# One token block of the forward gated layer moved from the first stage to the second

## The chip, the cores and the metric

The kernel runs on one core of a Trainium2 chip. A core has a matrix engine (TensorE, PE in the profile), a vector engine (VectorE, DVE), a scalar engine (ScalarE, ACT), GpSimd (POOL) and SyncE (SP), each with its own in-order queue of instructions, and 16 DMA engines. PEld is TensorE's weight load, which overlaps its matmuls. The metric is the device time of one execution in microseconds (us), taken as the median of several runs.

## The reference

The kernel computes a forward pass and all its gradients in one launch. S = 2048 tokens, D = 512 channels, F = 1376 hidden columns, bfloat16.

```python
x = A_q;  xn = layernorm(x)
# A: shift convolution, then a long causal convolution over the tokens
k_shift = sum over t < 4 of k[s - t] * shift_k[:, t]
kv = k_shift * v
y  = fft_conv(kv, ssm_k) + kv * ssm_D
s  = xn * y
# B: gated layer
g = xn @ w_gate;  u = xn @ w_up
h = sigmoid(g) * u
z = h @ w_down
out = x + s * silu(z)
# returned: out, and the gradients of A_q, A_k, A_v, shift_k, ssm_k, ssm_D,
#           w_gate, w_up, w_down for a given grad_out
```

## The kernel before

The 2048 tokens are 16 blocks of 128, numbered 0 to 15: token p*16 + j is partition p of block j. The long convolution works on four groups (cg) of 128 channels, each over all tokens, as dense Fourier matrices.

**Stage A** runs four streams side by side: `strG`, the forward part of the gated layer for the token blocks in the list `FA` (L34); and for each channel group `strK` (transform of the filter), `strV` (shift convolution and transform of kv) and `strX` (product and inverse transform, which gives y). `run_streams` (L519, called at L996) merges them into one program order by progress: `strG` is to run from 5% to 70% of the stage, with a total of `len(FA) * 11776` columns.

A forward block, `f_gen(i)` (L719), is 88 matmuls of 128x128 by 128 columns in three parts, each part followed by a sigmoid on ScalarE and a multiply on VectorE out of PSUM. On the way it loads, normalizes and transposes later blocks: `f_x` (three places ahead), `f_ln` (two), `f_xnT` (one, four transposes). Its results h and sigma are 352 KB each.

**Stage B** (`stepB`, L1133) takes the token blocks 0 to 15 in order. For each it does the down projection and the gates (`z_gen`, L1054), the gradient of the hidden layer (`d_gen`, L1085) and of x (`x_gen`, L1110); and, where block i + 3 was not in `FA`, that block's `f_gen` as well. Of the blocks done in stage A the last three (`LAG`, L30) stay in SBUF; the others, `NSP` of them, are written to DRAM at the end of `f_gen` and read back by `f_ld` (L752) in stage B. All of h and the two hidden gradients are also transposed by DMA and stored for the weight gradients.

**Stage C** runs the backward convolution (`frontC`, `backC`) beside the weight gradients (`dW`, L1189), which are 35 accumulations over the 16 token blocks that depend on nothing in stage C and also run alone at the end.

The order on the engines isn't the program order: `Rec.order` (L352) collects all operations with their dependencies, and places them one by one in the queue of their engine by estimated durations and by their number in the program; operations with two forms, the copies out of PSUM (`evac`, L241) and the normalization, go to ScalarE or VectorE as it finds them free. So an edit of the program order makes a new order of everything behind it. Because all operations are emitted by one line, every row of the profile names L515.

The lines that the change touches, and what depends on them:

```python
FA = [14, 13, 12, 11, 9, 7, 5, 4, 0, 1, 2]             # L34
NSP = len(FA) - LAG                                     # L35
SEQ = FA + [i for i in range(NJ) if i not in FA]        # L36: order of all forward blocks
POS = {i: n for n, i in enumerate(SEQ)}                 # L37
...
if n < NSP:                                             # L747, end of f_gen
    nc.gpsimd.dma_start(hF_d[n]..., hT)
    nc.gpsimd.dma_start(sF_d[n]..., sigT)
...
f = f_gen(i + LAG) if i + LAG < NJ and i + LAG not in FA else iter(())   # L1136, stepB
...
if i + LAG in FA[:NSP]:                                 # L1151
    f_ld(i + LAG)
```

Of the kernel before, what the change touches and what calls it, by code (L numbers as in the profile page):

```python
# [30 lines left out]
LATE = 0.25  # L31
SURE = 0.6
AHEAD = 500
FA = [14, 13, 12, 11, 9, 7, 5, 4, 0, 1, 2]  # L34
NSP = len(FA) - LAG  # L35
SEQ = FA + [i for i in range(NJ) if i not in FA]  # L36
POS = {i: n for n, i in enumerate(SEQ)}  # L37
# [481 lines left out]
def run_streams(streams, until=None):  # L519

    live = [list(st) + [0.0] * (5 - len(st)) for st in streams]
    while live:
        if until is not None and until():
            break
        for st in sorted(live, key=lambda s: s[2] + (s[3] - s[2]) * s[4] / s[1]):
            try:
                c = next(st[0])
            except StopIteration:
                live.remove(st)
                break  # L530
            if c:
                st[4] += c
                break
        else:
            raise RuntimeError("all streams blocked")
    return live
# [75 lines left out]
def kernel_impl(ctx, tc, A_q, A_k, A_v, A_shift_k, A_ssm_k, A_ssm_D, B_x, B_w_gate, B_w_up, B_w_down,  # L612
# [106 lines left out]
    def f_gen(i):  # L719
        n = POS[i]  # L720
        if n == 0:
            f_xnT(i)
            yield 512
        xnT = T[i]["xnT"]
        if n + 3 < NJ:
            f_x(SEQ[n + 3])
        sigT, hT = sig_r.next(), h_r.next()
        T[i]["sig"], T[i]["h"] = sigT, hT
        for pi, (f0, nb) in enumerate(FBS):
            if PS["wide"]:  # L730
                ps = ps_mm([2, 4, 128], name="psGU")
                pg, pu = ps[:, 0], ps[:, 1]
            else:
                pg, pu = ps_mm([4, 128], name="psG")[:], ps_mm([4, 128], name="psU")[:]
            for pt_, w in ((pg, wg), (pu, wu)):
                for b in range(nb):
                    for db in range(4):
                        nc.tensor.matmul(pt_[:, b, :], w[:, db, (f0 + b) * 128:(f0 + b + 1) * 128], xnT[:, db, :],
                                         start=(db == 0), stop=(db == 3))
            nc.scalar.activation(sigT[:, f0:f0 + nb, :], pg[:, 0:nb, :], ACT.Sigmoid)  # L740
            nc.vector.tensor_tensor(hT[:, f0:f0 + nb, :], pu[:, 0:nb, :], sigT[:, f0:f0 + nb, :], ALU.mult)
            if pi == 0 and n + 2 < NJ:
                f_ln(SEQ[n + 2])
            if pi == 1 and n + 1 < NJ:
                f_xnT(SEQ[n + 1])
            yield nb * 1024 + (512 if pi == 1 else 0)
        if n < NSP:  # L747
            nc.gpsimd.dma_start(hF_d[n].rearrange("p (a t) -> p a t", t=128), hT)
            nc.gpsimd.dma_start(sF_d[n].rearrange("p (a t) -> p a t", t=128), sigT)
        token_major(hT, hS_d[i])  # L750

    def f_ld(i):  # L752
        n = POS[i]
        sigT, hT = sig_r.next(), h_r.next()
        T[i]["sig"], T[i]["h"] = sigT, hT
        nc.gpsimd.dma_start(hT, hF_d[n].rearrange("p (a t) -> p a t", t=128))
        nc.gpsimd.dma_start(sigT, sF_d[n].rearrange("p (a t) -> p a t", t=128))
# [66 lines left out]
    def strG():  # L824
        for n, i in enumerate(FA):
            if n > 0:
                run_pend(2)
            yield from f_gen(i)
# [81 lines left out]
    def strK():  # L910
        for cg in range(NG):
            KT = stA.pop(("KT", cg))
            nc.vector.tensor_tensor(KT[:, 0:1], KT[:, 0:1], Dcol_b[:, cg:cg + 1], ALU.add)
            KC = KC_r.next()
            for jh in range(2):
                pt = ps_tr([8, 128], name="ps_kt")
                for jj in range(8):
                    nc.tensor.transpose(pt[:, jj, :], KT[:, 8 * jh + jj:S:16], ident)
                nc.evac(KC[:, 8 * jh:8 * jh + 8, :], pt[:], 1024)
                yield 1024  # L920
            if cg + 1 < NG:
                ld_KT(cg + 1)
            Qg = QgK_r.next()
            yield from step1(lambda j: KC[:, j, :], Qg)
            while cg > 1 and ("s3K", cg - 2) not in flags:
                yield 0
            Qf = QfK_r.next()
            yield from flip(Qg, Qf)
            stA["QfK", cg] = Qf
            flags.add(("flK", cg))  # L930

    def strV():
        for cg in range(NG):
            kh, vg = stA["kh", cg // 2], stA["vg", cg // 2]
            lc = (cg % 2) * GW
            c0, c1 = cg * GW, (cg + 1) * GW
            acc = acc_r.next()
            for lag in (3, 2, 1, 0):
                src = kh[:, 3 - lag: 3 - lag + NJ, lc:lc + GW]
                skl = skb[:, lag:lag + 1, c0:c1].to_broadcast([P, NJ, GW])  # L940
                if lag == 3:
                    nc.vector.tensor_tensor(acc, src, skl, ALU.mult)
                else:
                    term = term_r.next()
                    nc.vector.tensor_tensor(term, src, skl, ALU.mult)
                    yield 1024
                    nc.vector.tensor_tensor(acc, acc, term, ALU.add)
                yield 1024
            nc.gpsimd.dma_start(ksh_d[cg], acc.rearrange("p j d -> p (j d)"))
            kvt = kvt_r.next()  # L950
            nc.vector.tensor_tensor(kvt, acc, vg[:, :, lc:lc + GW], ALU.mult)
            if cg == 1:
                ld_k(1)
                ld_v(1)
            yield 1024
            Qg = QgV_r.next()
            yield from step1(lambda j: kvt[:, j, :], Qg)
            while cg > 0 and ("s3V", cg - 1) not in flags:
                yield 0
            Qf = QfV_r.next()  # L960
            yield from flip(Qg, Qf)
            stA["QfV", cg] = Qf
            flags.add(("flV", cg))

    def strX():
        yield from gen_ci()
        for cg in range(NG):
            while ("flK", cg) not in flags:
                yield 0
            QfK = stA.pop(("QfK", cg))  # L970
            KFg = KFg_r.next()
            for qq in range(4):
                yield from step3(QfK, qq, X_RI, KFg[:, qq])
                nc.gpsimd.dma_start(KK_d[cg, qq, :, 0], KFg[:, qq])
            flags.add(("s3K", cg))
            while ("flV", cg) not in flags:
                yield 0
            QfV = stA.pop(("QfV", cg))
            Bg = Bg_r.next()
            ys = {}  # L980
            for qq in range(5):
                if qq < 4:
                    Xc, Xs, Y = Xc_r.next(), Xs_r.next(), Y_r.next()
                    yield from step3(QfV, qq, X_RI, Xc)
                    nc.gpsimd.dma_start(KK_d[cg, qq, :, 1], Xc)
                    nc.vector.tensor_tensor(Y, Xc, KFg[:, qq], ALU.mult)
                    yield from step3(QfV, qq, X_IR, Xs)
                    nc.vector.tensor_tensor(Xs, Xs, KFg[:, qq], ALU.mult)
                    ys[qq] = ((Y, R_A), (Xs, R_B))
                    if qq == 3:  # L990
                        flags.add(("s3V", cg))
                if qq > 0:
                    yield from inv3(ys.pop(qq - 1), qq - 1, Bg)
            yield from inv1(Bg, y2A[:, :, cg * GW:(cg + 1) * GW])

    run_streams([(gG, len(FA) * 11776, 0.05, 0.7), (strK(), 4 * 10240, 0.0, 0.7), (strV(), 4 * 16384, 0.0, 0.8),  # L996
                 (strX(), 4 * 24576 + 4096, 0.2, 1.0)])
# [27 lines left out]
    def b_ld(i):  # L1025
        T[i]["x"], T[i]["go"] = xq2_r.next(), go_r.next()
        nc.gpsimd.dma_start(T[i]["x"], qC[:, i, :])
        nc.gpsimd.dma_start(T[i]["go"], goC[:, i, :])
# [104 lines left out]
    def stepB():  # L1133
        yield from z_gen(0)
        for i in range(NJ):
            f = f_gen(i + LAG) if i + LAG < NJ and i + LAG not in FA else iter(())  # L1136
            d, x = d_gen(i), x_gen(i)
# [11 lines left out]
            if i + 2 < NJ:  # L1149
                b_ld(i + 2)  # L1150
            if i + LAG in FA[:NSP]:  # L1151
                f_ld(i + LAG)
# [299 lines left out]
```

## Time and profile before

| | us |
|---|---|
| median of 5 runs | 557.92 (557.53 to 563.25) |
| the profiled execution | 557.02 |
| its span, first to last instruction | 555.1 |
| stage A, to the first matmul of token 0's backward | 176.4 |
| TensorE busy in the span | 525.3 |
| VectorE busy | 442.9 |
| ScalarE busy | 354.7 |
| mean granted TensorE clock | 0.999 |

The span is what the profile covers; the profiled execution's own time is 1.9 us longer, and 0.9 us under the median. "Busy" of TensorE counts overlapping matmuls as one stretch, so 95% busy isn't 95% of its peak. Stretches of time are counted from the first instruction; each operation of the program can be found in the trace by its place in its engine's queue.

### The profile page before, as it was taken

The numbers are of one execution on the slowest core, as the hardware profiler recorded it, in microseconds if no ns is written. First come the engines' busy times: TensorE is split into PE (matmuls) and PEld (weight loads), VectorE is DVE, ScalarE is ACT, GpSimd is POOL, SyncE is SP. The second block draws the span as 40 slices with busy tenths as digits, with TensorE's granted clock in tenths as the row PEclk, the third lists the DMA queues.
The fourth block names the chain that finished last, engine by engine and source line by source line (L and its number), as shares of the span: only waits on it lengthen the run. The fifth ranks groups of instructions, "written<-read, shape, count | busy, mean of one in ns | idle before, by whom it ended". The sixth has DMA issues, their size and how long they took to land.

```text
span 555.1 us, 13618 instructions
## 1 busy us (share of the span) xinstructions
PE 525.3 (95%) x5548; PEld 377.0 (68%) x5613; DVE 442.9 (80%) x869; ACT 354.7 (64%) x463; POOL 143.9 (26%) x254
## 2 busy tenths in 40 slices
PE   3987999999989999999999999999999999999996
PEld 2986998898868666667755665656756746667444
DVE  9599999957877999989899899648669798898510
ACT  7979999978986434354433444368848759775211
POOL 3243425303222122222232110310241051421221
PEclk9999999999999999999999999999999999999999
DMA  8978988967352899979999999998596369687431
GB/s 288 247 213 241 329 217 280 202 194 236 113 181 73 181 242 203 234 163 256 210 264 264 257 228 259 320 293 220 192 295 214 136 201 322 201 258 250 150 113 37
DMA packets 125608, 121.81 MB, mean 219 GB/s; under 512 B 75027, under 2 KB 104553, under 8 KB 125546
## 3 DMA queue, kind: packets, MB, share of 16 engines
q1 hardware_dynamic: 109946, 71.22, 51.8%
q0 software_dynamic: 15072, 49.72, 28.0%
q8 instruction: 44, 0.72, 0.5%
q14 instruction: 18, 0.15, 0.1%
q10 hardware_dynamic: 528, 0.00, 0.0%
HBM read 54.95 MB, written 48.27 MB: 186 GB/s over the span
## 4 chain that ended last, share of the span: by engine, by line
PE 67%; DVE 14%; issue 9%; ACT 6%; POOL 2%; DMA 2%; POOLq 0%; ACTq 0%; DVEq 0%
PE psum L515 67%; DVE slab L515 14%; ACT slab L515 6%; DMA out_dram<-slab 2%; POOL out_dram L515 1%; POOL slab L515 0%; ACT L515 0%; POOLq L1447 0%; POOLq L515 0%; ACTq L515 0%; DVEq L515 0%; POOLq L1436 0%
## 5 line engine op out<-in xcount | busy, mean ns | idle before, releaser
L515 PE MATMUL psum<-slab 128*128 128x128 bf16 (+4 forms) x5548 | 525.3, 255 | 25.4 <-ACT slab L515 12.7
L515 PEld LDWEIGHTS <-slab 128*128 128x128 bf16 (+3 forms) x5613 | 377.0, 102 | 173.3 <-issue 20.3
L515 DVE TENSOR_TENSOR slab<-slab 128x512 bf16<-128x512 bf16 (+6 forms) x507 | 293.6, 621 | 22.1 <-ACT slab L515 14.4
L515 ACT CAST slab<-psum 128x1024 bf16<-128x1024 f32 (+4 forms) x262 | 216.4, 872 | 81.9 <-PE psum L515 71.9
L515 ACT COPY slab<-psum 128x1024 bf16<-128x1024 bf16 (+1 forms) x89 | 76.8, 876 | 86.3 <-PE psum L515 86.0
L515 POOL DMA_DIRECT2D out_dram<-slab x75 | 44.4, 592 | 191.5 <-ACT slab L515 99.6
L515 DVE TENSOR_TENSOR slab<-psum,slab 128x512 bf16<-128x512 f32 (+2 forms) x68 | 44.4, 654 | 25.6 <-PE psum L515 14.9
L515 ACT ACTIVATE slab<-slab 128x512 bf16<-128x512 bf16 (+3 forms) x45 | 35.9, 803 | 17.5 <-DVE slab L515 17.1
L515 ACT ACTIVATE slab<-psum 128x512 bf16<-128x512 f32 (+1 forms) x64 | 37.4, 588 | 9.5 <-PE psum L515 8.1
L515 DVE SCALAR_TENSOR_TENSOR slab<-slab 128x1 f32<-128x1 f32 (+3 forms) x64 | 27.9, 436 | 12.3 <-ACT slab L515 11.5
L515 DVE CAST slab<-psum 128x1024 bf16<-128x1024 f32 (+1 forms) x27 | 31.3, 1162 | 4.3 <-PE psum L515 3.9
L515 POOL DMA_DIRECT2D KK_d<-slab x32 | 17.4, 545 | 61.0 <-ACT slab L515 33.7
L515 DVE COPY slab<-psum 128x1024 bf16<-128x1024 bf16 (+2 forms) x27 | 16.1, 610 | 14.1 <-PE psum L515 14.0
L515 POOL DMA_DIRECT2D slab<-in_A_q_dram x29 | 16.2, 558 | 38.1 <-DMA out_dram<-slab 22.0
L515 DVE TENSOR_SCALAR slab<-slab 128x1 f32<-128x1 f32 (+7 forms) x73 | 20.7, 319 | 0.4 <-PE psum L515 0.2
L515 DVE SCALAR_TENSOR_TENSOR slab<-psum,slab 128x512 f32<-128x512 f32 x16 | 10.9, 684 | 7.0 <-PE psum L515 6.9
L515 POOL DMA_DIRECT2D slab<-in_grad_out_dram x16 | 8.9, 558 | 28.3 <-DMA out_dram<-slab 18.3
L515 POOL TENSOR_TENSOR slab<-slab 128x1 f32<-128x1 f32 x16 | 12.0, 752 | 11.9 <-DVE slab L515 11.6
L515 POOL DMA_DIRECT2D slab<-in_A_k_dram x12 | 10.2, 850 | 3.0 <-PE psum L515 2.7
L515 DVE BATCH_NORM_STATS2 slab<-slab 128x6 f32<-128x512 bf16 x16 | 10.8, 678 | 0.0
L515 POOL DMA_DIRECT2D slab<-slab x8 | 4.4, 554 | 21.7 <-issue 21.7
L515 POOL DMA_DIRECT2D sF_d<-slab x8 | 4.3, 540 | 14.8 <-ACT slab L515 14.4
(21 smaller groups left out, 41.9 us busy)
## 6 DMA issues: line engine op xcount, KB each, us to landing
KK_d<-slab POOLq DMA_DIRECT2D x32, 256.0 KB, 3.2
slab<-KK_d SPq DMA_DIRECT2D x16, 512.0 KB, 5.0
out_dram<-slab POOLq DMA_DIRECT2D x58, 128.0 KB, 3.9
hS_d<-slab SPq DMA_DIRECT2D x16, 352.0 KB, 3.1
dgS_d<-slab SPq DMA_DIRECT2D x16, 352.0 KB, 4.0
duS_d<-slab SPq DMA_DIRECT2D x16, 352.0 KB, 4.2
slab<-hS_d SPq DMA_DIRECT2D x8, 512.0 KB, 5.6
slab<-dgS_d SPq DMA_DIRECT2D x8, 512.0 KB, 5.3
```

What stands on the lines that cost most here:

```text
L515: getattr(getattr(self.nc, eng), meth)(*[place(v) for v in a], **{x: place(v) for x, v in k.items()})
```

## The change

The list of the token blocks whose forward part is done in stage A loses one entry, block 12:

```diff
@@ -31,7 +31,7 @@
 LATE = 0.25
 SURE = 0.6
 AHEAD = 500
-FA = [14, 13, 12, 11, 9, 7, 5, 4, 0, 1, 2]
+FA = [14, 13, 11, 9, 7, 5, 4, 0, 1, 2]
 NSP = len(FA) - LAG
 SEQ = FA + [i for i in range(NJ) if i not in FA]
 POS = {i: n for n, i in enumerate(SEQ)}
```

What follows from it:

- Stage A has ten forward blocks instead of eleven. Block 12's `f_gen` runs in stage B, in the iteration of token 9. The blocks left to stage B are 3, 6, 8, 10, 12 and 15 instead of 3, 6, 8, 10 and 15.
- `NSP` falls from 8 to 7: block 12's h and sigma are neither written to DRAM nor read back (two stores and two loads of 352 KB).
- Every forward block behind block 13 moves one place forward in `SEQ`, with its load, normalization and transposes.
- The total of `strG` that `run_streams` works with is 10 x 11776 instead of 11 x 11776, so the remaining blocks are spread over the same part of the other streams.
- `Rec.order` makes a new order of all engines from the forward part of block 13 on.

No operation but those four DMA transfers is added or removed.

## Prediction

> **What bounds the kernel now.** I began with the page's first lines, to see which engine has no slack over the whole span.
>
> ```profile
> PE 525.3 (95%) x5548; PEld 377.0 (68%) x5613; DVE 442.9 (80%) x869; ACT 354.7 (64%) x463; POOL 143.9 (26%) x254
> ...
> PE psum L515 67%; DVE slab L515 14%; ACT slab L515 6%; DMA out_dram<-slab 2%; POOL out_dram L515 1%; POOL slab L515 0%; ACT L515 0%; POOLq L1447 0%; POOLq L515 0%; ACTq L515 0%; DVEq L515 0%; POOLq L1436 0%
> ```
>
> TensorE (PE) is busy 95% and holds 67% of the chain. The change neither adds nor removes a matmul, so the time can move only where PE stands still. Hence the second view, busy time by stretch. I cut it at stage A (to about 176 us) and stage B (176 to about 357); after that the weight gradients fill whatever is left, and the last 43 us hold hardly anything but them.
>
> ```profile
> core 0: us, PE busy (x) PEld busy (x) DVE busy (x) ACT busy (x) POOL busy (x), PEclk, DMA share, GB/s
> ...
> 30.00:36.00 6.00, 5.85 (x99) 5.50 (x99) 6.00 (x8) 3.80 (x7) 3.54 (x5) 1.00 0.58 203
> 36.00:43.00 7.00, 5.01 (x77) 4.63 (x78) 7.00 (x14) 6.08 (x9) 2.23 (x4) 1.00 0.80 222
> 43.00:85.00 42.00, 38.60 (x596) 35.70 (x599) 38.19 (x64) 41.04 (x50) 14.68 (x26) 1.00 0.89 267
> 85.00:110.00 25.00, 23.43 (x336) 20.38 (x338) 23.30 (x43) 24.57 (x32) 10.66 (x17) 1.00 0.90 241
> 110.00:140.00 30.00, 29.79 (x459) 27.33 (x463) 19.62 (x25) 24.37 (x32) 7.47 (x14) 1.00 0.73 210
> 140.00:171.00 31.00, 28.20 (x364) 22.73 (x368) 24.91 (x36) 28.73 (x33) 6.14 (x12) 1.00 0.37 122
> ...
> 512.00:555.20 43.20, 38.49 (x222) 20.25 (x223) 11.84 (x16) 9.02 (x16) 10.46 (x17) 0.99 0.31 98
> ```
>
> Columns: length, then busy us (instructions) of PE, PEld, DVE, ACT, POOL, then PE clock, DMA share, GB/s. Read stage A as three regimes. From 43 to 110 ScalarE (ACT) is full: 41.04 of 42, 24.57 of 25. From 110 to 140 PE is: 29.79 of 30. From 140 to 171 neither is, and the end of the convolution decides. Before that, 30 to 36 is token block 12 on PE, almost alone (99 matmuls), with ACT busy 3.80 of 6.
>
> Third, two pairs of token iterations of stage B with a forward block in them, and one pair without (the starts are the gate sigmoids of tokens 5, 7, 9 and 11, at 225.4, 250.1, 274.9 and 295.3):
>
> ```profile
> 225.40:250.10 24.70, 24.59 (x255) 16.92 (x255) 21.96 (x57) 11.17 (x19) 6.36 (x11) 1.00 0.86 191
> 250.10:274.90 24.80, 24.69 (x257) 17.02 (x257) 21.99 (x56) 10.65 (x19) 6.73 (x12) 1.00 1.08 236
> 274.90:295.30 20.40, 19.70 (x167) 12.01 (x167) 19.50 (x52) 7.99 (x15) 5.50 (x10) 1.00 1.18 244
> ```
>
> PE is full in the first two (24.69 of 24.80), nearly so in the third (19.70 of 20.40).
>
> **What one block costs an engine.** Rows of the 30 to 36 stretch by form:
>
> ```profile
> L515 PE MATMUL psum<-slab 128*128 128x128 bf16 x98 | 5.7, 219 | 0.0
> ...
> L515 ACT ACTIVATE slab<-psum 128x512 bf16<-128x512 f32 x2 | 1.2, 600 | 1.2 <-PE psum L515 1.2
> ...
> L515 ACT ACTIVATE slab<-slab 128x512 bf16<-128x512 bf16 x1 | 0.8, 804 | 0.0
> ...
> L515 ACT COPY slab<-psum 128x512 bf16<-128x512 bf16 x1 | 0.6, 587 | 0.4 <-PE psum L515 0.4
> ...
> L515 ACT ACTIVATE slab<-psum 128x384 bf16<-128x384 f32 x1 | 0.5, 491 | 0.3 <-PE psum L515 0.3
> ```
>
> 98 matmuls in 5.7 us are 58 ns each. A block is 88 matmuls and 4 transposes: 92 x 58 ns = 5.3 us of PE. ACT: 1.2 + 0.8 + 0.6 + 0.5 = 3.1 us. VectorE (DVE): three multiplies out of PSUM (0.69 + 0.69 + 0.55) and the layernorm pieces (0.68 + 0.18 + 0.15 + 0.15), also 3.1 us.
>
> **Step 1: stage B gets the block.** In the changed program's instruction order block 12 stands in tokens 8 and 9, in the hole that the third pair above partly covers. The price is the difference of the pairs: 24.8 - 20.4 = **+4.4 us**. It is under 5.3 because 20.40 - 19.70 = 0.7 us of PE idle is filled; DVE, at 19.50 of 20.40, has 0.9 us left for about 2.5 us more, but the pair as a whole grows and the two pairs with a block show that DVE then fits (21.99 of 24.80). Bounds: 3.9 (all the idle of both tokens filled, and the idle of a neighbour) to 5.3 (none).
>
> **Step 2: stage A loses it.** The list also has every later block one place earlier and the written order is made anew, so I count matmuls and 1024-wide PSUM evacuations (about 1.03 us each on ACT, 1.22 or 0.69 on DVE) between the same events of the convolution in both orders, and price each slice by the engine that is full there. "cg" is a group of 128 channels.
> - To the first matmul on group 0's kv (now at 42.8 us): 36 matmuls more (+2.1 us), three ACT evacuations more (+3.1 us). Idle PE and ACT of 30 to 43 take some of it: +2.2 taken, bounds 0 and +3.1.
> - From there to the end of cg 0 (now 85.0; ACT full): five ACT evacuations and two sigmoids fewer, 5 x 1.03 + 2 x 0.6 = -6.3; by DVE's smaller loss it would be -3.6. I take -6.0, as ACT is at 41.04 of 42 and DVE at 38.19.
> - cg 1 (to 122.1; ACT full for most of it): two ACT evacuations more, +2.0; nine matmuls more. Bounds +0.5, +2.0; I take +2.0.
> - cg 2 (to 153.2; mostly PE full): 37 matmuls fewer, 37 x 58 ns = -2.1.
> - cg 3 (to 170.2): 21 matmuls more and two DVE evacuations more, +1.2 to +2.4; I take +1.3.
> - To the first matmul of token 0's backward (176.4): 17 matmuls fewer, -1.0.
>
> Sum: 2.2 - 6.0 + 2.0 - 2.1 + 1.3 - 1.0 = **-3.6 us**. As a check, the totals ahead of stage B fall by 89 matmuls (5.2 us) and some 2.8 us each on ACT and DVE, so -3.6 lies between what an evacuation-limited and a PE-limited stage would return.
>
> **Step 3: the spill.** Block 12's h and sigma no longer go to DRAM and back: two stores and two loads of 352 KB, 4 POOL issues of 0.54 us, 1.4 of 121.8 MB. I cost it at nothing: ACT's waits that end on a DMA are 1.7 us in all, POOL is 26% busy. If the loads' place did matter (DMA share 1.18 in the third pair), it is a gain below 0.7 us, that pair's PE idle. The block's transposing DMA moves into stage B; SP issues nothing there that PE waits for within the pair.
>
> **Step 4: stage C.** The matmuls are the same and the order differs a little. PE is 161.21 of 164.00 from 348 to 512, so a gain is at most 2.8; the one larger wait of that stretch (PE is 18.38 of 20.00 from 440 to 460) may double or go. I take 0, bounds -1.5 and +2.
>
> **Sum.** +4.4 - 3.6 = +0.8 us. The profiled execution took 557.0 us (span 555.1), so 557.8; the median of the runs, 557.9, is 0.9 higher, which gives **558.7 us**. A measurement of this kernel tells about 1%, 5.6 us, from no change; this is none.
>
> [...] Less filler in stage A means longer PE gaps. The row first: from 20 to 176 us PE's longest wait is 1.2 us and the granted clock is 1.00 in every stretch shown. [...]
>
> **Rivals.**
> - *Slower: DVE ends the cg 0 slice.* DVE is 7.00 of 7 from 36 to 43 and 38.19 of 42 after. If the 1.2 us kv multiplies rather than ACT set that slice, it returns 3.6 instead of 6.0, and the later start (+2.2, up to +3.1) stays: stage A gives back 0.3 to 1.2, the total is +3.2 to +4.1, about 561 to 562; with the block at its full 5.3 us, 563. It decides once DVE's idle in that slice is under ACT's. With stage C's +2 it passes 1%. Against it: ACT's 98%.
> - *Faster: the early start is free.* ACT has 2.2 + 0.9 us idle in 30 to 43, just the three evacuations that come earlier. Then the first term is 0 instead of +2.2, and stage A gives back 5.8: -1.4, or 556.5; with stage C's -1.5, 555. Against it: DVE is full there, and the three evacuations need PE's matmuls first.
> - *The list entry changes nothing but names:* the block costs the same 5.3 us of PE wherever PE is full. For it: 110 to 140. Then B's 4.4 meets 5.3, 557.0.
>
> **Chances.** My forecast, with the third rival inside it (557 to 560): 0.45. Slower rival (560 to 565): 0.30. Faster (553.5 to 557): 0.22. Something else: 0.03. The range, 554.5 to 564.0, reaches into both. Of the slower case two thirds stay within 1%, of the faster two thirds or more: faster 0.08, same 0.71, slower 0.21.
>
> **What would show it.** Right: the pair of tokens 8 and 9 lengthens by 4 to 5 us; stage B starts 3 to 4 us before 176.4; ACT is still full from about 45 to 110; PE's clock stays 1.00; stage C keeps its length. Wrong: stage B starts no earlier than 175, or before 171; or a new wait of over 2 us in stage C.

## Result

| | before | after |
|---|---|---|
| median of all runs shown, us | 558.22 (66 runs) | 556.22 (34 runs) |
| lowest run, us | 556.73 | 555.38 |
| the profiled execution, us | 557.02 | 555.96 |
| its span, us | 555.1 | 554.2 |

The ratio of the times is 0.9951 with a 95% interval of 0.9939 to 0.9963; it is taken between the means (556.1 and 558.8 us), and one execution of before, 565.65 us, is left out as disturbed. The changed kernel is about half a per cent faster. The forecast was 558.7 us, 0.8 us above the median of before's first five runs (557.92). The time lies in the forecast's range (554.5 to 564.0), but on the other side of before.

The first lines of the page after, busy time and the chain that ended last:

```profile
PE 526.9 (95%) x5553; PEld 377.4 (68%) x5613; DVE 444.8 (80%) x867; ACT 354.0 (64%) x465; POOL 139.8 (25%) x250
...
PE psum L515 63%; DVE slab L515 15%; ACT slab L515 8%; POOL out_dram L515 1%; DMA slab<-in_grad_out_dram 1%; POOL slab L515 1%; DMA KK_d<-slab 0%; ACT L515 0%; POOLq L1447 0%; POOL ksh_d L515 0%; POOL hF_d L515 0%; POOLq L515 0%; DVEq L515 
```

Nothing has changed in kind: TensorE is still busy 95% of the span, and TensorE's matmuls are most of the chain. Where the time went has to be read by stretch. First stage A of after, from the first kv matmul (it starts at 45.2, the load of its weights at 45.1) to the end of group 0 (81.5), and on through the two later regimes:

```profile
45.10:81.40 36.30, 32.97 (x499) 29.81 (x500) 34.12 (x59) 34.57 (x43) 11.83 (x21) 1.00 0.90 264
81.40:110.00 28.60, 26.03 (x376) 22.84 (x379) 26.53 (x43) 28.42 (x36) 10.49 (x19) 1.00 0.86 243
110.00:140.00 30.00, 29.27 (x445) 26.50 (x447) 17.85 (x25) 24.76 (x32) 5.89 (x11) 1.00 0.61 171
140.00:169.00 29.00, 26.80 (x349) 21.87 (x351) 25.52 (x35) 27.19 (x35) 6.56 (x13) 1.00 0.36 121
```

The columns here and below are those of the prediction's tables. The three regimes are those of before. ScalarE is nearly full to 110 (34.57 of 36.30, 28.42 of 28.60), PE from 110 to 140 (29.27 of 30), then neither. In before the first kv matmul starts at 43.8, after a wait:

```profile
42.43 0.61 PE L515 MATMUL psum<-slab 128*128 128x128 bf16 x8 [0.54 <-ACT slab L515]
43.83 1.35 PE L515 MATMUL psum<-slab 128*128 128x128 bf16 x20 [0.80 <-ACT slab L515]
```

From it to the end of group 0 (85.0) before took 41.2 us; after takes 36.2.

Then tokens 8 and 9 of stage B, from one gradient's first matmul to that of token 10. Before:

```profile
272.06:292.26 20.20, 19.50 (x161) 11.81 (x162) 18.52 (x49) 8.12 (x14) 6.05 (x11) 1.00 1.11 257
```

After:

```profile
268.53:293.27 24.74, 24.64 (x253) 16.94 (x254) 21.88 (x55) 10.59 (x18) 6.79 (x12) 1.00 0.95 228
```

Block 12 stands there with its 92 matmuls (253 against 161), and PE is full (24.64 of 24.74). The pair is 4.5 us longer.

Last, stage C: from the end of stage B to the end of groups 0 and 1, of group 2, of group 3, and to the end of the span (the stretches are cut 0.1 to 0.3 us ahead of the last matmul of each). Before:

```profile
361.60:448.70 87.10, 86.42 (x767) 56.31 (x779) 65.25 (x91) 63.76 (x71) 16.30 (x27) 1.00 0.72 213
448.70:484.80 36.10, 34.32 (x314) 22.42 (x319) 31.28 (x42) 28.17 (x32) 13.30 (x21) 1.00 0.85 269
484.80:521.60 36.80, 36.53 (x306) 23.55 (x310) 29.50 (x42) 20.82 (x25) 8.85 (x14) 1.00 0.79 246
521.60:555.10 33.50, 28.94 (x155) 14.96 (x154) 7.35 (x6) 6.06 (x12) 6.57 (x11) 0.99 0.22 71
```

After:

```profile
362.30:446.70 84.40, 83.72 (x756) 55.01 (x768) 63.65 (x87) 62.67 (x71) 17.06 (x27) 1.00 0.75 212
446.70:486.10 39.40, 39.03 (x336) 24.73 (x342) 34.98 (x46) 28.96 (x32) 12.39 (x21) 1.00 0.90 278
486.10:522.80 36.70, 36.44 (x305) 23.30 (x309) 29.45 (x43) 20.73 (x26) 8.87 (x15) 1.00 0.70 218
522.80:554.20 31.40, 26.89 (x145) 13.95 (x144) 7.16 (x6) 5.42 (x11) 6.54 (x11) 0.97 0.23 71
```

Take length less PE's busy time, row by row. Before: 0.68, 1.78, 0.27, 4.56. After: 0.68, 0.37, 0.26, 4.51. All of the difference, 1.4 us, is in the group 2 slice. PE's busy time is moved between the slices (2.70 us out of the first, 2.05 out of the last, 4.71 into group 2's) and its sum is the same, 186.2 and 186.1. Stages A and B together end 0.7 us later than before, stage C with the tail takes 191.9 us instead of 193.5 by these rows, and the span falls by 0.9.

**What PE waited for in group 2.** PE's waits from 348 to 512 in before are one line. Columns: what waited and for what, us in total, times, longest:

```profile
PE psum L515 <- ACT slab L515: 1.5, 1, 1.5
```

After has no wait there that the view lists. PE's and ScalarE's timeline of before at that place (start, us, engine, operation, in brackets the idle time before it and what ended it):

```profile
458.19 5.98 PE L515 MATMUL psum<-slab 128*128 128x128 bf16 x57 [1.47 <-ACT slab L515]
...
457.13 7.02 ACT L515 CAST slab<-psum 128x1024 bf16<-128x1024 f32 x8 [1.73 <-DMA out_dram<-slab]
```

And GpSimd's queue ahead of it:

```profile
447.44 1.20 POOL L515 DMA_DIRECT2D slab<-in_A_v_dram  x1 [1.41 <-issue]
448.64 1.73 POOL L515 DMA_DIRECT2D out_dram<-slab  x2
```

In the order of cause: the filter gradient of group 1, 512 KB, is ready at 445.85. Its store (`nc.gpsimd.dma_start(out_5...)`, L1307) stands in GpSimd's queue behind a load of v (447.44, 1.20 us), and is issued at 448.64. It lands at 457.05, 8.4 us later. The filter gradient's tile is a view of the buffer `B1` (`dKT = ar.view(B1_r.blks[0][0]...)`, L1297), into which ScalarE is to copy the next group's result out of PSUM. That result is complete at 451.9, but ScalarE, free since 455.4, waits 1.73 us for the landing, and PE, whose PSUM isn't freed, 1.47.

In after the same store is issued at 448.45 and lands at 457.97, no sooner; ScalarE starts that copy at 458.45. PE's timeline there is one unbroken group:

```profile
445.83 20.39 PE L515 MATMUL psum<-slab 128*128 128x512 bf16 x150
```

So the store is not faster. The new order has 4.7 us more of matmuls in this slice, most of them weight gradients, and they cover the wait.

### The profile page after: what moved, and what is told of

It is laid out like the page before. It is cut to its first block, busy times and chain, and to the rows that moved or that the text cites. A ratio compares the mean times of both kernels' runs of the same rounds, so it can differ in the third digit from the quotient of the medians.

```text
span 554.2 us, 13609 instructions
## 1 busy us (share of the span) xinstructions
PE 526.9 (95%) x5553; PEld 377.4 (68%) x5613; DVE 444.8 (80%) x867; ACT 354.0 (64%) x465; POOL 139.8 (25%) x250
## 4 chain that ended last, share of the span: by engine, by line
PE 63%; DVE 15%; issue 10%; ACT 8%; POOL 2%; DMA 1%; POOLq 0%; DVEq 0%; ACTq 0%
PE psum L515 63%; DVE slab L515 15%; ACT slab L515 8%; POOL out_dram L515 1%; DMA slab<-in_grad_out_dram 1%; POOL slab L515 1%; DMA KK_d<-slab 0%; ACT L515 0%; POOLq L1447 0%; POOL ksh_d L515 0%; POOL hF_d L515 0%; POOLq L515 0%; DVEq L515 0%; ACTq L515 0%; POOLq L1436 0%
## 5 line engine op out<-in xcount | busy, mean ns | idle before, releaser
L515 PEld LDWEIGHTS <-slab 128*128 128x128 bf16 (+2 forms) x5613 | 377.4, 102 | 171.9 <-issue 17.6
L515 DVE TENSOR_TENSOR slab<-slab 128x512 bf16<-128x512 bf16 (+5 forms) x507 | 293.2, 621 | 13.6 <-ACT slab L515 6.4
L515 ACT COPY slab<-psum 128x1024 bf16<-128x1024 bf16 (+2 forms) x90 | 75.5, 862 | 90.4 <-PE psum L515 90.1
L515 DVE COPY slab<-psum 128x1024 bf16<-128x1024 bf16 (+1 forms) x26 | 17.1, 666 | 12.6 <-PE psum L515 12.3
L515 POOL TENSOR_TENSOR slab<-slab 128x1 f32<-128x1 f32 x16 | 10.8, 676 | 14.6 <-DVE slab L515 14.3
L515 POOL MEMSET slab<- 1x384 bf16 (+4 forms) x14 | 5.7, 417 | 8.8 <-DVE slab L515 7.4
```

Of the source, the lines that this page charges most:

```text
L515: getattr(getattr(self.nc, eng), meth)(*[place(v) for v in a], **{x: place(v) for x, v in k.items()})
```

## Experiments

Theory 1: the exchange of a block between the stages comes out at about nothing, and the gain is stage C's wait for the store, which the new order happens to cover. Theory 2: fewer blocks in stage A, with less written to DRAM, are faster by themselves.

In the runs whose names begin with n_, the 48 transposing DMAs are plain copies of the same size; the transposition is left out, so the three weight gradients are formed from untransposed blocks. The order of all engines is the same. All that these runs share is shown here once:

```diff
-            nc.sync.dma_start_transpose(st.rearrange("p (a b) -> p a b", b=128), srcT.rearrange("p a t -> p (a t)"))
+            nc.sync.dma_start(st, srcT.rearrange("p a t -> p (a t)"))
```

**Before and after again** (no edit).

> The kernel before once more, for a second profiled execution of it. Theory 1 (the moved block costs 0.7 us by the end of stage B; the gain is in stage C, where TensorE waited for ScalarE, and that for the landing of a store of the filter gradient, and no longer does): stage B ends at 361.6 us again within 0.3; if this execution is longer than the first one's 557.0, the excess stands behind 440 us, at that wait. Theory 2 (the gain is in stages A and B, by fewer blocks and less spill traffic there): the excess stands in front of 362. Ratio 1.000 in both.

> The changed kernel once more. Theory 1: token 0's backward starts at 172.4 within 0.3, stage B ends 0.7 later than in the kernel before, no TensorE wait over 0.6 us from 348 to 512; ratio 0.995. Theory 2: the end of stage B is earlier than before's in most executions, by some 2 us; ratio 0.995.

Before gave 559.27 us, ratio to before 1.0017 (0.9988 to 1.0046); after gave 556.05, ratio 0.9948 (0.9921 to 0.9974). In the profile of before PE waits at the same place, 1.9 us this time, with the store landing at 457.31. The difference between the kernels and the wait come again, and stage B ends where it did (361.7 against 361.8).

**The store on another queue.** In both kernels the store of the filter gradient, one of 512 KB for each of the four groups, is issued by SyncE; nothing in the order of PE, VectorE or ScalarE moves:

```diff
-            nc.gpsimd.dma_start(out_5[c0:c1, :], dKT.rearrange("p n j -> p (n j)"))
+            nc.sync.dma_start(out_5[c0:c1, :], dKT.rearrange("p n j -> p (n j)"))
```

> The kernel before with the stores of the filter gradient issued by SyncE instead of GpSimd; the orders on TensorE, VectorE and ScalarE are the same to the last instruction. Theory 1: the store of group 1 is issued near 446 instead of 448.6 and lands 2 to 4 us earlier than 457, TensorE's wait of 1.5 us there goes: 1.5 to 2.5 us less, ratio 0.9955 to 0.9975. Theory 2: nothing in stages A and B is touched, ratio 1.000.

> The changed kernel with the same edit. Theory 1: there is no wait left to remove, so it is as the changed kernel within 0.5 us, ratio 0.995, and 0 to 1 us slower than the kernel before with that edit. Theory 2: ratio 0.995, and 2.5 us faster than the kernel before with that edit.

Before with this line: 556.05 us, ratio 0.9968 (0.9931 to 1.0005). After with it: 556.21, ratio 0.9951 (0.9923 to 0.9979), as after without. The timeline of before with the line, SyncE, ScalarE and PE at the same place:

```profile
446.67 0.34 SPq L515 DMA_DIRECT2D out_dram<-slab  x1
...
455.18 8.11 ACT L515 CAST slab<-psum 128x1024 bf16<-128x1024 f32 x9 [0.69 <-PE psum L515]
...
453.66 10.65 PE L515 MATMUL psum<-slab 128*128 128x512 bf16 x96
```

The store is issued 2.0 us sooner (446.67 against 448.64), ScalarE no longer waits for a DMA, and PE runs through; when the store lands the trace doesn't say. The last weight gradient's matmul starts at 549.4 us, as in after (549.4), instead of 550.3. Eleven blocks without the wait are as fast as ten at the median. After has nothing to gain from it, because its wait was covered. The interval of the first ratio still reaches 1: four of the 12 runs took 559.1 to 562.8 us, the other eight 555.1 to 556.1. So the step was made again with plain copies.

**The plain copies by themselves**, before and after, and then the store's queue in the first of them.

> The kernel before with a plain DMA copy of the same 352 KB in place of each of the 48 DMA transposes: the transposition is left out, so the three weight gradients are computed from untransposed blocks; the order on every engine is the same to the last instruction. Theory 1 (the moved block costs 0.7 us by the end of stage B, the gain is a wait for the landing of a store in stage C): TensorE does not wait for these transfers, so stage B ends at 361.6 within 1 us and the wait near 457 is there. Long executions (over 1.5 us above the shortest) stay if they come from the loads and stores on GpSimd's queue, and go if the transposes make them.

> The changed kernel with plain copies for the transposes in the same way. Theory 1: stage B ends 0.7 later than in the kernel before with plain copies, TensorE has no wait over 1 us in stage C, the whole is 1 to 3 us shorter. Theory 2 (gain in stages A and B from fewer blocks and spills): stage B ends earlier than there.

> The kernel before with plain copies and the filter gradient's stores issued by SyncE; the orders on TensorE, VectorE and ScalarE are the same. Theory 1a (the base gain is TensorE's wait for this store, the long executions come from it too): 1.5 to 2.3 us shorter than the kernel before with plain copies at the median, all 12 executions within 1.5 us. Theory 1b (the long executions come from the dk store, whose landing releases VectorE at 482 us): the same gain at the short end, but a third to a half of the executions still long. Theory 2 (stages A and B): no gain.

The three gave 558.45 us, ratio 0.9995 (0.9969 to 1.0021); 556.18, ratio 0.9953 (0.9930 to 0.9976); and 556.17, ratio 0.9935 (0.9910 to 0.9961). The plain copies change neither kernel's time, and moving this store takes 2.3 us off the first, to the time of the second. All 12 runs of `n_sp5_before` lie within 1.3 us; of `n_before`'s, five lie 1.8 us or more above its lowest. Group 2's slice of `n_sp5_before`, as it was cut for before:

```profile
449.40:483.80 34.40, 34.08 (x314) 22.37 (x319) 31.15 (x42) 28.18 (x32) 12.11 (x19) 1.00 0.87 270
```

The same 314 matmuls as in before (36.10 us with 34.32 of them busy), without the idle time.

**Three more profiles of `n_before`,** for its longer executions, and to see how its profile varies.

> The kernel before with plain copies once more, for a profile of one of its long executions (5 of 12 timed ones were 559.4 to 560.1, the others 557.6 to 558.5). Theory 1: the excess stands in stage C between 448 and 490 us, at the transfers that have no reserve there: the filter gradient's store, the halo copies, the dk store. Theory 2: in front of 362.

> The kernel before with plain copies, a further profile for the same question: in a long execution, theory 1 has the excess between 448 and 490 us, theory 2 in front of 362.

> The kernel before with plain copies, a further profile for the same question: in a long execution, theory 1 has the excess between 448 and 490 us, theory 2 in front of 362.

They took 557.63, 558.60 and 558.11 us; none was a long one, so neither theory was put to the test. PE's wait for the store was there each time, 1.9, 1.7 and 1.6 us. What also varied is when everything starts: the first kv matmul came at 44.0, 44.8 and 44.8 (43.8 in before's own profile, 44.9 in `n_before`'s), and the whole timeline kept that shift. Its cause is in the stretch from 15 to 18 us. Two rows of before:

```profile
16.00:17.00 1.00, 1.00 (x22) 1.00 (x20) 0.07 (x1) 1.00 (x2) 0.22 (x1) 1.00 1.19 313
17.00:18.00 1.00, 1.00 (x22) 1.00 (x20) 1.00 (x2) 1.00 (x2) 0.00 (x0) 1.00 1.17 236
```

The same of `n_before`, whose order is the same:

```profile
16.00:17.00 1.00, 1.00 (x12) 1.00 (x11) 0.00 (x0) 1.00 (x2) 0.23 (x1) 1.00 1.23 314
17.00:18.00 1.00, 1.00 (x13) 1.00 (x10) 0.13 (x1) 0.61 (x1) 0.00 (x0) 1.00 1.11 261
```

PE is full in both, but runs about half as many matmuls. Their starts are 107 ns apart until 15.2 us in before and until 18.0 in `n_before`, and 56 ns from then on. In the 19 profiles the moment lay between 15.1 and 18.0. The granted clock in the rows reads 1.00 all the while, but each trace's own record of the clock begins only at that moment (15.3 in before, 18.0 in `n_before`); 107 ns is also the spacing that a row with a granted clock of 0.50 has, under "The spill" below. So this is read here as the matmul clock going from half to full, and called the clock step; what sets its moment was not shown.

So two profiles should be compared at the same moment of this step. Two pairs can be, to 0.2 us: `n_sp5_before` with after (16.7 and 16.6), and `n_look1` with `sp5_after` (15.4 and 15.2). In the first pair the last matmul of stage B starts at 362.5 in both, and the last matmul of all at 549.3 and 549.4. In the second it is at 361.9 in both, and then 550.8 against 549.1. The exchange of the block is worth nothing, to a tenth or two of a microsecond. The wait in stage C is worth 1.7 us.

**The spill.** After, with the three blocks that stay in SBUF also written to DRAM at the end of their `f_gen`, so six stores of 352 KB more. In the first form they are part of the program, which is ordered anew; in the second they are put into GpSimd's queue with the order otherwise kept:

```diff
-        if n < NSP:
+        if n < NST:            # n_spill: NST = len(FA)
...
+        elif n < len(FA):      # n_spill_fix: behind the operation recorded last
+            nc.extra[len(nc.ops) - 1] = [... the two stores, to a buffer of their own ...]
```

> The changed kernel with plain copies, and h and sigma of the three blocks that stay in SBUF written to DRAM as well (six more stores of 352 KB that nobody reads, three times what the change saves in stores). Theory 1: within 0.7 us of the changed kernel with plain copies. Theory 2: 2 us or more slower.

> The changed kernel with plain copies and six more stores of 352 KB (h and sigma of the three blocks that stay in SBUF), put behind the instructions that make the data without the order of any other instruction being changed. Theory 1 (spill traffic costs nothing; the 3.3 us of the earlier run with these stores came from the order): within 0.5 us of the changed kernel with plain copies. Theory 2: 2 us or more slower.

They gave 559.44 us, ratio 1.0025 (1.0004 to 1.0047), and 561.66, ratio 1.0053 (1.0034 to 1.0073). By the time alone both are theory 2; the traces say otherwise. In `n_spill` the times are those of `n_after`, 0.4 us late from the start, up to 134 us, and the loss comes between 134 and 177. There the new order leaves PE idle 2.1 us longer (4.9 against 2.8), with 4.1 us of waits for ScalarE instead of 2.2, and no wait of PE, VectorE or ScalarE in that stretch ends on a store. In `n_spill_fix` four of the six stores, 1.4 MB, were issued before 134 us, and up to there it is only 0.1 us behind `n_after`. The rest of the 5.5 us begins with one wait, VectorE's:

```profile
139.40 0.56 DVE L516 TENSOR_TENSOR slab<-psum,slab 128x384 bf16<-128x384 f32 x1 [6.04 <-DMA eF_d<-slab]
```

This is block 2's last multiply. The last two added stores had come to stand ahead of it in the queues, so it had to wait until they had read its tile: a fault of this experiment, not a cost of the bytes. PE stood still with it for 4.5 us, and what followed shows in its clock (a row of PE's timeline, then two stretches):

```profile
140.02 4.67 PE L516 MATMUL psum<-slab 128*128 128x512 bf16 x52 [4.54 <-DVE slab L516]
140.00:143.07 3.07, 3.05 (x27) 2.78 (x27) 1.25 (x2) 1.74 (x2) 0.00 (x0) 0.50 0.01 4
143.07:146.00 2.93, 2.51 (x33) 1.99 (x33) 2.58 (x4) 2.46 (x4) 0.00 (x0) 1.00 0.00 0
```

The granted clock was 0.50 for the 3 us after that gap, with matmuls 107 ns apart, and 1.00 behind it, with 56 ns. Group 2's slice of stage A took 5.5 us more than in `n_after`, 4.2 of it idle time of PE and 1.2 more busy time. What remains of the experiment is that 1.4 MB of additional stores in stage A cost 0.1 us. The prediction's price for the spill, nothing, stands for that part; the loads that the change saves were not tried.

**Other lists.** Ten blocks with another one moved, nine blocks, and twelve:

```diff
-FA = [14, 13, 12, 11, 9, 7, 5, 4, 0, 1, 2]
+FA = [14, 12, 11, 9, 7, 5, 4, 0, 1, 2]              # n_fa_no13
+FA = [14, 13, 12, 9, 7, 5, 4, 0, 1, 2]              # n_fa_no11
+FA = [14, 13, 9, 7, 5, 4, 0, 1, 2]                  # n_fa9
+FA = [14, 13, 12, 11, 10, 9, 7, 5, 4, 0, 1, 2]      # n_fa12
```

> With plain copies, ten blocks in stage A, but block 13 is the one that goes to stage B, not 12. Theory 1: stage A is 3 to 5 us shorter than with eleven blocks, stage B 4 to 5 us longer, stage B ends within 1.5 us of the kernel before with plain copies; stage C gains or loses up to 2 us by the new order. Theory 2: as fast as the changed kernel within 0.7 us, since count and traffic are the same.

> With plain copies, ten blocks in stage A, with block 11 as the one that goes to stage B. Theory 1 (stages A and B exchange for -0.5 to +1.5 us, stage C is chance): end of stage B within 1.5 us of the kernel before with plain copies; the end of the kernel anywhere from 3 us shorter to 1 us longer. Theory 3 (ten blocks also make the better order in stage C): 1.5 to 3 us shorter, no wait of TensorE over 1 us behind 362, as with 12 or 13 moved.

> With plain copies, nine blocks in stage A: 12 and 11 both go to stage B. Theory 1: each block moved takes about 4 us from stage A and adds 4.4 to 5.0 to stage B (the second fills less idle time), so stage B ends 1 to 2.5 us later than in the changed kernel with plain copies; stage C's order is new, within 2 us either way: in all 0 to 3 us slower than that kernel. Theory 2 (fewer blocks in stage A are faster): 1 to 3 us faster than that kernel.

> FA with twelve blocks: block 10 joins stage A, plain copies in place of the 48 transposing DMAs. Theory 1 (the exchange between the stages nearly cancels, and the median moves with stage C's wait for the landing of the filter gradient's store): stage A is 3 to 6 us longer than with eleven blocks, the pair of tokens 6 and 7 is 4 to 5 us shorter, and the end of stage B moves by less than 2 us; the total is 556 to 557 if the order has no such wait and 558 to 560 if it has one, so the wait in the trace, not the number of blocks, tells which. Theory 2 (fewer blocks and less spill in stage A are faster by themselves): twelve blocks are slower than eleven by 2 us or more, 560.5 or above, with the loss in stage A.

| blocks in stage A | median, us | ratio to before (95%) | PE's wait for the store in stage C |
|---|---|---|---|
| 12 (`n_fa12`) | 558.00 | 0.9995 (0.9977 to 1.0013) | none |
| 11 (`n_before`) | 558.45 | 0.9995 (0.9969 to 1.0021) | 1.8 us |
| 11, store on SyncE (`n_sp5_before`) | 556.17 | 0.9935 (0.9910 to 0.9961) | none |
| 10, 12 moved (`n_after`) | 556.18 | 0.9953 (0.9930 to 0.9976) | none |
| 10, 13 moved (`n_fa_no13`) | 555.57 | 0.9937 (0.9915 to 0.9959) | none |
| 10, 11 moved (`n_fa_no11`) | 556.66 | 0.9945 (0.9920 to 0.9969) | none |
| 9 (`n_fa9`) | 559.42 | 1.0012 (0.9990 to 1.0035) | none; 0.8 us for a load of k |

Theory 2 falls on both sides: nine blocks are 3.2 us slower than ten (2.4 by the lowest runs; theory 1 had 0 to 3), and eleven are as fast as ten once the store's wait is gone. The exchange has a flat bottom at ten and eleven. For twelve, theory 1 had 556 to 557 us without a wait; it is 558.0, a miss by one. Against `n_sp5_before` (whose clock step is 0.5 us later) stage A grows by 6.0 us, the pair of tokens 6 and 7 falls only from 24.7 to 20.2, and the last matmul is 1.4 us later. With nine, against `n_after` (whose clock step is 1.0 us earlier), stage A gives back 2.3 us more, where theory 1 had 4, and stage B takes 4.5.

Only the list of eleven has the wait for the store, of the six lists. So the number of blocks does not decide that; each list is a new order, and one of them left the place open. `n_fa_no13` is the lowest of all, 0.6 us under `n_after` in the same runs. At nearly the same moment of the clock step (15.3, against 15.2 in `sp5_after`) its last matmul is 0.5 us earlier (548.6 against 549.1), 0.3 of it by token 15 of stage B. It beats before; its interval and `n_after`'s overlap.

**Another store on SyncE's queue too.** Besides the filter gradient's, the two 1 MB stores of the gradient of k:

```diff
-                nc.gpsimd.dma_start(o2C[:, :, c0 - GW:c1], stC["dk"])
+                nc.sync.dma_start(o2C[:, :, c0 - GW:c1], stC["dk"])
```

> The same, with the two dk stores of 1 MB issued by SyncE as well (the engines' orders are the same up to 515 us). Theory 1a: as n_sp5_before within 0.5 us. Theory 1b: no long executions left, all 12 within 1.5 us of the shortest. If long ones stay in a third of the executions, they come from neither store.

557.69 us, ratio 0.9977 (0.9959 to 0.9995): slower by 1.5 us than with the one store moved. The last matmul starts at 549.1 us (549.3 with the one), but the span is 555.3 instead of 554.0: from there to the end it takes 6.2 us instead of 4.7. So the loss comes behind the last matmul, where only the last stores are left; the engines' orders also differ from 515 us on. It is no cure for every store.

## Why the prediction was wrong

**Step 1, stage B gets the block: right.** +4.4 us for tokens 8 and 9 was forecast; the pair measured 20.2 and 24.7, +4.5, and PE is full there, as argued.

**Step 2, stage A loses it: right in sum in the pair of profiles, less so in its terms.** The middle column takes the two profiled executions; the right one takes `n_sp5_before` for before, whose clock step comes at the same moment as after's, to 0.1 us. Rows are rounded singly.

| slice | predicted | before to after | same clock step |
|---|---|---|---|
| to the first kv matmul | +2.2 | +1.4 | +0.7 |
| to the end of cg 0 | -6.0 | -5.0 | -4.9 |
| cg 1 | +2.0 | +1.5 | +1.5 |
| cg 2 | -2.1 | -1.0 | -0.9 |
| cg 3 | +1.3 | +0.6 | +0.6 |
| to token 0's backward | -1.0 | -1.6 | -1.6 |
| stage A | -3.6 | -4.0 | -4.7 |
| stage B, tokens 8 and 9 | +4.4 | +4.5 | +4.5 |
| stage B, other tokens | 0 | +0.2 | +0.2 |
| to the end of stage B | +0.8 | +0.7 | 0.0 |

The prediction's "now at 42.8 us" is where the weights of the first kv matmul are loaded; the matmul itself starts at 43.8 in before, and at 45.2 in after (weights at 45.1). So the first two terms were each about a microsecond too large, in opposite directions: the later start cost 1.4 us instead of 2.2, and group 0 gave back 5.0 instead of 6.0. That they cancel is luck. In cg 2 the matmuls fewer were worth half their forecast price: PE's busy time in the slice fell by 1.8 us, not 2.1, and its idle time grew by 0.8. And half of the first row's +1.4 comes from the clock step: before's profile had an early one, after's one in the middle. Without it stage A gave back 4.7 us, 1.1 more than forecast, and the exchange came to 0.0 instead of +0.8.

**Step 3, the spill: not contradicted** by the 1.4 MB of stores that cost 0.1 us.

**Step 4 is the step that failed.** "The matmuls are the same and the order differs a little", so stage C was taken as 0, with bounds of -1.5 and +2. It measured -1.6 in the pair of profiles, just past the lower bound. The place was seen ("the one larger wait of that stretch ... may double or go"), but it was left without a cause, and so without a sign. The cause stood in step 3: "ACT's waits that end on a DMA are 1.7 us in all" is one single wait, that of ScalarE for the store's landing at 457, and PE's wait of 1.5 us hangs on it. The prediction priced it under the spill and did not join the two. Of the six lists run, before's alone has this wait, and in its six profiles it is 1.5 to 1.9 us long: a new order was more likely to lose it than to double it. The likeliest value was below zero.

**The addition of 0.9 us for the median was wrong too.** Before's profile was 0.9 under the median of its runs, and this was carried over to after as if it belonged to the metric. After's profile is 0.3 under its median. Two things went with before's offset: its clock step was among the earliest, and its wait for the store, 1.5 us, the shortest of the profiles (1.6 to 1.9 in the others). Neither carries over to after.

The account of 558.7 against 556.2, 2.5 us, is then: stage C 1.6; the exchange 0.1; the offset 0.6 (0.9 carried over, 0.3 found); the remaining 0.2 is what lies around the span, and rounding.

**Rivals.** The time is that of the faster rival (555 to 556.5), but its mechanism only in part: the later first kv matmul cost 0.7 to 1.4 us, less than the 2.2 forecast but not nothing, and stage A gave back 4.0 to 4.7 us, not 5.8. Most of the distance to the forecast came from stage C, which this rival carried as a bound and not as its argument. The slower rival, in which VectorE ends the cg 0 slice, did not come about by its own sign: VectorE has 2.2 us idle there (34.12 of 36.30), ScalarE 1.7 (34.57). The margin was small, and the slice's 5.0 lies between that rival's 3.6 and the forecast's 6.0. Nor did stage A return the 5.3 us of the third. The longer gaps in PE that less filler was to bring did not come in after: PE's longest wait between 20 and 172 us is 1.0 us (1.2 between 20 and 176 in before), and the granted clock is 1.00 in every row shown of stages A and B. In `n_spill_fix` 4.5 us of idle time were followed by 3 us at a clock of 0.50.

**What stays open.** The medians fell by 2.0 us, the means by 2.8, the lowest runs by 1.35, and the one pair of profiles at the same clock step, with and without the wait, by 1.7. Before's runs spread upwards more than after's, which lifts its mean: 19 of 66 took over 559 us, and none of after's 34. The store's wait alone doesn't make these: in `sp5_before`, which is without it, four of 12 did, in `n_sp5_before` none. Of the 136 timed runs of before beside the experiments 43 took over 559 us, and 30 of these have a mean granted clock of 0.997 or less, which none of the other 93 has. 0.997 is also the mean of `n_spill_fix`'s profile, with its one stretch at 0.50, so a longer gap in PE may be in them; the profiles, all of lower runs, don't show it. Why the planner leaves the place in stage C open for one list of six stays open too.

## What to carry to other kernels

When work is moved between two stages that are both full, the exchange may come to nothing, and the time is decided by whichever wait the new order closes or opens elsewhere. Before taking a later stage as unchanged, list its few waits and follow each to what ends it; a wait that ends on the landing of a store into which the next result is to be written can be removed directly, here by one line, for as much as the whole change brought. And compare profiles only after lining up what varies from one execution to the next, or a microsecond of it is read as an effect.

## What was unexpected in the hardware

- The matmul rate at the start doubled (from 107 to 56 ns between starts) at a moment that varied in executions with the same order (15.2 us in before, 18.0 in `n_before`). Everything behind it shifted by up to 1.1 us (first kv matmul at 43.8 and 44.9), while the granted clock in the profile's rows read 1.00.
- After 4.5 us without a matmul in `n_spill_fix` the granted clock was 0.50 in the row from 140.00 to 143.07 us, with matmuls again starting 107 ns apart, and 1.00 in the row behind it.
- The landing of the same 512 KB store from GpSimd's queue took 8.4 us for group 1 in before (issued 448.64, landed 457.05) and 3.6 for group 2 (484.14, 487.75); in after 9.5 and 4.2. In before group 1's is issued between a 1 MB load and a 1 MB store of the same queue. Whether one of them makes it late was not tried; issued 2 us sooner from SyncE's queue, it held nobody up.
